# x is added to the early part of y by VectorE instead of TensorE, twelve idle matmuls are dropped, and the stage's entries are spread to its end

## The chip, the cores and the metric

The kernel runs on one core of a Trainium2 chip. The metric is the device time of one execution in microseconds (us); the time before is the median of three runs. Where a time inside an execution is given, it counts from the first instruction of the profiled execution.

Engines in the profile: PE is TensorE (matmuls), PEld its weight loads, DVE VectorE, ACT ScalarE, POOL GpSimd, SP SyncE. "Granted clock" is the share of its full clock that TensorE was given at that moment.

## The reference

```python
# attention with a causal window of 64, 8 batches x 8 heads, 576 rows, 64 columns
scores = scale * np.matmul(q, k.transpose(0, 1, 3, 2))
mask = (rel >= 0) & (rel < 64)
attn_out = softmax(where(mask, scores, -1e9)) @ v
x = attn_out.transpose(0, 2, 1, 3).reshape(8, 576, 512)
# spectral mix: 64 modes, a complex 512 x 512 matrix for each
X = np.fft.rfft(x, axis=1)
Yr = einsum('bmd,mde->bme', Xr, w_r) - einsum('bmd,mde->bme', Xi, w_i)
Yi = einsum('bmd,mde->bme', Xr, w_i) + einsum('bmd,mde->bme', Xi, w_r)
Y[:, :64] = Yr + 1j * Yi
y = np.fft.irfft(Y, n=576, axis=1)
u = x + y
out = u + np.maximum(u @ w_ch, 0.0)
```

## The kernel before

**The stream of weights.** The mode matrices `w_r` and `w_i` are 127 loads of 1 MB each (the imaginary part of mode 0 isn't needed), cast to 512 KB of bf16 on the way by GpSimd's DMA queue (`load_w`). They start during the attention and run until shortly before the output. Every load, numbered 0 to 126, is used by one call of `half(i)` (L533): 16 matmuls with the weights as the stationary operand and the modes of all batches, XQ, as 16 moving columns. The results gather in two PSUM banks, `psys`, and every eight modes are copied to `YT` (the first 48 modes, "early", 96 rows of real and imaginary parts) or to `YTl` (the last 16, "late", 32 rows).

**The slots.** After the attention, the loop variable `now` counts slots: `half(now)`, then `issue(now)` (L506), which issues the loads for which a buffer is free, then the functions that were put into `work[now]`. The order on PE, POOL, DVE and ACT is that of the program (`manual_schedule`). Slots 0 to 94 end with the last early mode: `S_I` is 95. Slots 95 to 124 (`T_I` is 125) are the stage that is changed. Halves 125 and 126 come behind it, in the tail.

**The buffers.** `ring` (L491) holds 14 places for weights: five of `wlate`, eight of `wmid` and, as the only one without a pool, the first half of XQ once its modes are used up (`view(XQ, ...)`). Work that needs room takes a place with `claim` and returns it with `give`; `taken` counts what is claimed in each slot, and `issue` doesn't issue a load that would leave too little for a later claim. `claim` prefers the XQ place when it is free.

**The stage's entries.** With the early modes known, the inverse transform of the early part is done while the late weights stream in. For each pair p of batches, 60 entries in all:
- `turn_first(b)` transposes a batch's `YT` (four matmuls of 128 columns), and VectorE copies it to `Yp[b]`; `channel_first(b)` multiplies it by `w_ch` (four matmuls of 512 columns), and ScalarE copies that.
- `make_u(p, t)` for row tiles t = 0 to 3: for the two batches, the inverse transform of the early part (one matmul each, stationary `trigI`), and x added to it by a second matmul each with a unit matrix (`ident_bf`, L727). ScalarE copies the 128x1024 sum to `U`. For t < 2, `U` is a claimed place; for t = 2 and 3 it lies over x itself, in rows of one batch that are read up to t = 3, so both copies are made after the last tile of x is read (`late_u`).
- `add_z(p, t)`: the same with the `w_ch` rows, and VectorE adds the result to `Z0`, which holds x @ w_ch from earlier slots.
- `last_tile(p, x)`: the last 64 rows of both batches at once, for Z (VectorE adds) and for u (ScalarE copies; x is added by a matmul with a permuted unit matrix).
- `drop(p)` returns two claimed places.

`make_u`, `add_z` and `last_tile` share two PSUM tiles of two banks each (`ps_e`, tag `pse`). L797 spreads the entries evenly over slots 95 to 122. In slots 122 and 123 six idle matmuls each (L840) use a further `ps_e` tile, `psd`.

**The tail.** The PSUM of the stage is given up and taken over by the tail's tiles. `lay` puts `Z0` of two tiles into PSUM, two idle matmuls follow, half 125, six idle matmuls, half 126 (L929 to L934). Then the late part is turned, multiplied by `w_ch`, and for each of 18 slot tiles added to Z (`late_rows`), rectified on ScalarE, completed by the late part of u, added to `U` on VectorE (`final`, L916) and written out by SyncE's queue.

Of the kernel before, what the change touches and what calls it, by code (L numbers as in the profile page):

```python
# [9 lines left out]
FP32 = mybir.dt.float32  # L10
# [3 lines left out]
ALU = mybir.AluOpType  # L14
# [6 lines left out]
def view(ap, off, dims):  # L21

    return bass.AP(ap.tensor, ap.offset + off, [list(ap.ap[0])] + [list(d) for d in dims])
# [3 lines left out]
def kernel(  # L27
# [10 lines left out]
    nc = tc.nc  # L38
    B, H, S, D = q.shape
    NM = moe_w_r.shape[0]  # L40
    DM = moe_w_ch.shape[0]
# [3 lines left out]
    NT = 5  # L45
# [23 lines left out]
    ident_bf = consts.tile([128, 128], BF16, name="ident_bf")  # L69
    ident_r = consts.tile([128, 128], FP32R, name="ident_r")  # L70
    trigF = consts.tile([128, NT, 2 * NM], BF16, name="trigF")
    x_sb = keep.tile([128, B // 2, 2 * NT, DM], BF16, name="x_sb")
# [3 lines left out]
    def block(b, t):  # L76

        return t if b % 2 == 0 else (t + 1) % NT

    def x_rows(b, t, n=128):  # L80
        return x_sb[:n, b // 2, (b % 2) * NT + block(b, t), :]
# [32 lines left out]
    NLOAD = 2 * NM - 1  # L114
# [5 lines left out]
    def load_w(i, pool, tag, wt=None):  # L120
        m, im = divmod(i + (i > 0), 2)
        if wt is None:
            wt = pool.tile([128, NC, DM], BF16, name="wt", tag=tag)
        src = moe_w_i if im else moe_w_r
        nc.gpsimd.dma_start(out=wt, in_=src[m].rearrange("(p c) e -> p c e", c=NC))  # L125
        wtiles[m, im] = wt
# [28 lines left out]
    with tc.tile_pool(name="tmpf", bufs=1, side="right") as tmp:  # L155
# [6 lines left out]
        for t0, t1 in ((0, 3), (3, NT)):  # L162
            n = t1 - t0
            mt = tmp.tile([128, 2, n * NM], FP32, name="mtf")
            nc.vector.tensor_tensor(out=view(mt, 0, [[NM, n], [1, NM]]), in0=view(mo, 0, [[0, n], [1, NM]]),
                                    in1=view(to, t0, [[1, n], [0, NM]]), op=ALU.mult)
# [188 lines left out]
    nw = 0  # L355
# [38 lines left out]
    with tc.manual_schedule(engines={mybir.EngineType.PE, mybir.EngineType.Pool}):  # L394
# [11 lines left out]
        for b in range(1, B):  # L406
            start = -(-9 * (b - 1) // 2)
# [12 lines left out]
        for w in range(NWIN + 1):  # L420
# [5 lines left out]
            n = len(todo)  # L426
# [16 lines left out]
            if w in (NWIN - 4, NWIN - 1):  # L443
                i = (B - 2) % 2 if w == NWIN - 4 else (B - 1) % 2
# [4 lines left out]
            if w in (NWIN - 4, NWIN):  # L449
                i = (B - 2) % 2 if w == NWIN - 4 else (B - 1) % 2  # L450
# [17 lines left out]
    E0 = 96  # L468
# [16 lines left out]
    turns_bf = late2.tile([128, 64, 2], BF16, name="turns_bf")  # L485
# [5 lines left out]
    ring = [(i, wlate, "wl", None) for i in range(LW)]  # L491
# [4 lines left out]
    S_I = 2 * L0 * MG - 1  # L496
    T_I = NLOAD - 2
    work = {}
    taken = [0] * (NLOAD + 1)

    def put(i, f, delta=0):
        work.setdefault(i, []).append(f)
        for j in range(i, NLOAD + 1):
            taken[j] += delta

    def issue(i):  # L506
        nonlocal nw
        while nw < NLOAD:
            ring.sort(key=lambda r: (max(r[0], i), r[1] is not None, r[0]))
            if ring[0][0] > i:  # L510
                return
            held = [r[0] for r in ring if r[0] > i] + [nw]
            if any(sum(x > j for x in held) + taken[j] > places for j in range(i, nw + 1)):
                return
            _, pool, tag, ap = ring.pop(0)
            load_w(nw, pool, tag, ap)
            ring.append((nw, pool, tag, ap))
            nw += 1

    now = 0  # L520

    def claim(name, dtype=FP32R):
        ring.sort(key=lambda r: (r[0], r[1] is None))
        r = ring.pop(0)
        assert r[0] <= now, (name, now, ring)
        if r[1] is None:
            return r[3].rearrange("p c e -> p (c e)").bitcast(dtype).rearrange("p (a e) -> p a e", a=2), r
        return r[1].tile([128, 2, DM], dtype, name=name, tag=r[2]), r

    def give(c):  # L530
# [2 lines left out]
    def half(i):  # L533
        m, im = divmod(i + (i > 0), 2)
        w = wtiles.pop((m, im))
        psy = psys[m // MG % 2 if m < NM - 1 else 0]
        off = (m % MG) * NC * 2 * B if m < NM - 1 else 0
        own = m % MG == 0 or m == NM - 1
        for e in range(NC):
            for c in range(NC):  # L540
                nc.tensor.matmul(out=view(psy, off + 2 * B * e, [[1, 2 * B]]),  # L541
                                 lhsT=w[:, c, 128 * e:128 * e + 128],
                                 rhs=XQ[:, m // HM, c, :, 1 - im:3 - im, m % HM],
                                 start=own and not im and e == 0 and c == 0,
                                 stop=c == NC - 1 and (im == 1 or m == 0), skip_group_check=True)
        if (im or not m) and (m % MG == MG - 1 or m == NM - 2):
            g, n = m // MG, m % MG + 1
            for ri in range(2 if m < NM - 1 else 0):
                if g < L0:
                    dst = view(YT, g * 2 * MG + ri * MG, [[E0, NC], [NC * E0, B], [1, n]])  # L550
                else:
                    dst = view(YTl, (g - L0) * 2 * MG + ri * MG, [[B * R, NC], [R, B], [1, n]])
                evac(dst, view(psy, ri, [[2 * B, NC], [2, B], [NC * 2 * B, n]]), ri)
# [144 lines left out]
    Yp, U = {}, {}  # L698

    def spent(k):  # L700

        return view(YT, 2 * DM * k, [[DM, 2], [1, DM]])

    def turn_first(b):
        Yp[b] = claim("Yb") if b < B - 2 else (spent(b - B + 2), None)
        psa = ps_a.tile([128, NC, 128], FP32R, name="psa")
        for e in range(NC):
            nc.tensor.transpose(out=psa[:E0, e, :], in_=YT[:, b, e, :], identity=ident_r)
        nc.vector.tensor_copy(out=Yp[b][0][:E0, 0, :], in_=psa[:E0].rearrange("p c e -> p (c e)"))

    def channel_first(b):
        psw = ps_a.tile([128, DM], FP32, name="psw")
# [5 lines left out]
    def first_rows(ps, b, t, k, x):  # L718

        parts = [(b, 128 * t)] if t < NT - 1 else [(b, 513), (b + 1, 512)]  # L720
        for n, (bb, o) in enumerate(parts):
            last = n == len(parts) - 1
            nc.tensor.matmul(out=ps, lhsT=trigI[:E0, o:o + 128], rhs=Yp[bb][0][:E0, k, :],  # L723
                             start=n == 0, stop=last and not x)
        if x:
            perm = ident_bf if t < NT - 1 else view(turns_bf, 0, [[1, 128]])
            nc.tensor.matmul(out=ps, lhsT=perm, rhs=x_rows(b, t), start=False, stop=True)  # L727

    def add_z(p, t):
        ps = ps_e.tile([128, 2, DM], FP32, name="pse", tag="pse")  # L730
# [2 lines left out]
        z = Z0[:, 4 * p + t]  # L733
        nc.vector.tensor_tensor(out=z, in0=ps, in1=z, op=ALU.add)  # L734

    late_u = []

    def make_u(p, t):
        ps = ps_e.tile([128, 2, DM], FP32, name="psf", tag="pse")
        for j in range(2):  # L740
            first_rows(ps[:, j, :], 2 * p + j, t, 0, True)
        if t < 2:
            U[4 * p + t] = claim("U", FP32)[0]
            nc.scalar.copy(out=U[4 * p + t], in_=ps)
            return
        U[4 * p + t] = x_sb[:, p, NT * (t - 2) + t - 2:NT * (t - 2) + t + 2, :].bitcast(FP32).rearrange(
            "p (j h) e -> p j (h e)", j=2)
        late_u.append((4 * p + t, ps))
        if t == 3:
            for s, q in late_u:  # L750
                nc.scalar.copy(out=U[s], in_=q)
            late_u.clear()

    def last_tile(p, x):
        ps = ps_e.tile([128, 2, DM], FP32, name="psg", tag="pse")
# [16 lines left out]
    items = []  # L772

    def first_of(b, k):
        if b < B:
            items.append((lambda: (turn_first, channel_first)[k](b), 1 - k if b < B - 2 else 0))

    def step(f, *a, delta=0):
        items.append((lambda: f(*a), delta))
# [4 lines left out]
    for p in range(NP):  # L784
        for t in range(3):
            step(add_z, p, t)
            step(make_u, p, t, delta=t < 2)
        first_of(2 * p + 2, 0)
        step(make_u, p, 3)
        first_of(2 * p + 2, 1)  # L790
        step(add_z, p, 3)
        step(last_tile, p, False)
        step(last_tile, p, True)
        step(drop, p, delta=-2 if p < NP - 1 else 0)
        first_of(2 * p + 3, 0)
        first_of(2 * p + 3, 1)
    for k, (f, delta) in enumerate(items):  # L797
        put(S_I + k * (T_I - 2 - S_I) // len(items), f, delta)
    places = len(ring)

    def out_of(s):
# [6 lines left out]
    def idle(o, n):  # L808
        for _ in range(n):
            nc.tensor.matmul(out=o, lhsT=ident_bf, rhs=view(trigF, 0, [[1, DM]]), start=True, stop=True)  # L810

    E = mybir.EngineType
    with tc.manual_schedule(engines={E.PE, E.Pool, E.DVE, E.Activation}):
# [16 lines left out]
        with ExitStack() as pe:  # L830
            ps_a = pe.enter_context(tc.tile_pool(name="ps_a", bufs=1, space=PSUM, reuse_waits="tile"))
            ps_e = pe.enter_context(tc.tile_pool(name="ps_e", bufs=2, space=PSUM, reuse_waits="tile"))
            for now in range(S_I, T_I):
                half(now)
                issue(now)
                for f in work.get(now, []):
                    f()
                if T_I - 3 <= now < T_I - 1:
                    psd = ps_e.tile([128, 2, DM], FP32, name="psd", tag="pse")
                    idle(psd[:, 0, :], 6)  # L840
        now = T_I
        assert nw == NLOAD

# [7 lines left out]
        for h in range(2):  # L851
            left = [[4 * (2 * h + k) + t for t in range(4)] for k in range(2)]
            for _ in range(8):
# [6 lines left out]
                k = 1 - kind[-2] if len(kind) > 1 and kind[-2] is not None else (0 if not kind else 1)  # L860
                k = k if left[k] else 1 - k
# [58 lines left out]
        def pool(name, stack=p2, **kw):  # L920
# [15 lines left out]
                              in_=view(psys[0], 0, [[2 * B, NC], [2, B], [1, 2]]))  # L936
# [58 lines left out]
```

## Time and profile before

| | us |
|---|---|
| median of 3 runs | 431.09 |
| the three runs | 431.09, 430.18, 436.92 |
| the profiled execution's own time | 434.36 |
| its span, first to last instruction | 432.3 |
| PE busy | 355.8 (82%) |
| PEld busy | 234.6 (54%) |
| DVE busy | 186.1 (43%) |
| ACT busy | 160.9 (37%) |
| POOL busy | 91.6 (21%) |
| mean granted clock of TensorE | 0.791 |

The profiled execution is one execution; its time is compared with nothing but itself and the median of the runs. Busy shares are means over stages with different limits. In the view by slices each digit is the busy share of a fortieth of the span in tenths (9 is 90% or more); PEclk is the granted clock in tenths. In the chain of waits a row is the start, the length and the work that the end of the program followed from at that time: a transfer from its issue to its landing, or instructions of an engine. In the view by groups a row is line, engine, operation, tiles, shape and count, then busy us, mean ns of one, and the engine's idle time before it. "x16" is a count of instructions, and a matmul's length in the records holds its way through the array, so that successive ones overlap.

### The profile page before, as it was taken

The numbers are of one execution on the slowest core, as the hardware profiler recorded it, in microseconds if no ns is written. First come the engines' busy times: TensorE is split into PE (matmuls) and PEld (weight loads), VectorE is DVE, ScalarE is ACT, GpSimd is POOL, SyncE is SP. The second block draws the span as 40 slices with busy tenths as digits, with TensorE's granted clock in tenths as the row PEclk, the third lists the DMA queues.
The fourth block names the chain that finished last, engine by engine and source line by source line (L and its number), as shares of the span: only waits on it lengthen the run. The fifth ranks groups of instructions, "written<-read, shape, count | busy, mean of one in ns | idle before, by whom it ended". The sixth has DMA issues, their size and how long they took to land.

```text
span 432.3 us, 11457 instructions
## 1 busy us (share of the span) xinstructions
PE 355.8 (82%) x5148; PEld 234.6 (54%) x5167; DVE 186.1 (43%) x340; ACT 160.9 (37%) x252; POOL 91.6 (21%) x174
## 2 busy tenths in 40 slices
PE   6989998999989667595867768677879899999982
PEld 2555665666654567373645545455546555655431
DVE  5466866776763202173334332111114523351685
ACT  4485866866754100041211120101124222331672
POOL 6131321331111404331221212212212110300000
PEclk9999999999997555597656565765659955899896
DMA  8999999999999999999999999999999999992598
GB/s 143 212 214 214 212 213 213 212 213 213 213 213 203 191 214 180 257 213 213 213 213 214 214 213 213 214 215 213 213 213 213 214 214 213 213 213 50 214 349 313
DMA packets 30352, 91.96 MB, mean 213 GB/s; under 512 B 2784, under 2 KB 2784, under 8 KB 30304
## 3 DMA queue, kind: packets, MB, share of 16 engines
q0 software_dynamic: 25344, 81.80, 95.3%
q1 hardware_dynamic: 4960, 9.44, 5.8%
q8 instruction: 40, 0.66, 0.5%
q14 instruction: 8, 0.07, 0.0%
HBM read 162.53 MB, written 9.44 MB: 398 GB/s over the span
## 4 chain that ended last, share of the span: by engine, by line
PE 45%; DMA 37%; DVE 8%; issue 5%; ACT 3%; POOL 1%; DVEq 0%; POOLq 0%; ACTq 0%
DMA wt<-in_moe_w_r_dram 13%; DMA wt<-in_moe_w_i_dram 12%; DMA XQ<-in_moe_w_r_dram 9%; PE pso L318 6%; PE psy L541 6%; PE pst L221 5%; PE psv L238 3%; PE psx L340 3%; DVE x_sb L326 3%; PE pss L275 2%; DMA wch<-in_moe_w_ch_dram 2%; PE pss L374 2%; PE pss L876 2%; PE pss L294 2%; PE psf L723 2%
## 5 line engine op out<-in xcount | busy, mean ns | idle before, releaser
L541 PE MATMUL psy<-XQ,wt 128*128 128x16 bf16 x1680 | 64.7, 191 | 33.3 <-DMA wt<-in_moe_w_i_dram 16.0
L541 PEld LDWEIGHTS <-wt 128*128 128x128 bf16 x1680 | 55.6, 104 | 64.4 <-DMA wt<-in_moe_w_i_dram 27.4
L682 PE MATMUL psz<-wch,xT 128*128 128x512 f32 x144 | 63.7, 584 | 5.6 <-DMA wch<-in_moe_w_ch_dram 5.6
L685 ACT CAST Z<-psz 128x1024 fp32r<-128x1024 f32 x18 | 18.2, 1012 | 101.0 <-PE psz L682 87.0
L676 DVE CAST xT<-pxt 128x1024 fp32r<-128x1024 bf16 x18 | 22.0, 1225 | 71.8 <-PE pxt L671 71.7
L125 POOL DMA_DIRECT2D wt<-in_moe_w_r_dram x54 | 29.1, 540 | 82.1 <-DMA wt<-in_moe_w_r_dram 34.4
L125 POOL DMA_DIRECT2D wt<-in_moe_w_i_dram x51 | 27.6, 542 | 84.8 <-DMA wt<-in_moe_w_i_dram 38.9
L300 ACT ACTIVATE et<-pss 128x512 bf16<-128x512 f32 x72 | 39.2, 600 | 13.4 <-PE pss L294 12.3
L682 PEld LDWEIGHTS psz<-wch,xT 128*128 128x128 f32 x144 | 36.2, 278 | 11.5 <-issue 5.7
L318 PE MATMUL pso<-vt,et 128*64 128x65 bf16 (+1 forms) x576 | 33.1, 206 | 4.0 <-DVE x_sb L326 3.1
L734 DVE TENSOR_TENSOR Z<-pse,Z 128x1024 fp32r<-128x1024 f32 x16 | 19.6, 1224 | 33.9 <-PE pse L723 33.9
L318 PEld LDWEIGHTS <-et 128*64 128x64 bf16 (+1 forms) x576 | 22.7, 111 | 16.0 <-issue 8.0
L326 DVE TENSOR_TENSOR x_sb<-pso,rcp 128x640 bf16<-128x640 f32 x32 | 26.3, 822 | 0.9
L275 PE MATMUL pss<-band,ident_bf 64*64 64x512 bf16 x160 | 21.2, 410 | 1.4 <-ACT et L300 1.4
L59 DVE COPY vT<-pst 128x768 bf16<-128x768 bf16 x16 | 15.3, 957 | 13.5 <-PE pst L221 13.5
L909 ACT ACTIVATE pss<-pss 128x1024 f32<-128x1024 f32 (+1 forms) x18 | 17.3, 960 | 5.5 <-PE pss L885 4.8
L59 DVE CAST YT<-psy 128x256 fp32r<-128x256 f32 x6 | 2.5, 424 | 38.5 <-PE psy L541 38.5
L294 PE MATMUL pss<-qT,kT 64*64 64x128 bf16 (+1 forms) x640 | 15.6, 218 | 0.6 <-issue 0.6
L58 ACT COPY vt<-psv 128x768 bf16<-128x768 bf16 x16 | 12.9, 808 | 8.5 <-PE psv L238 8.4
L671 PE MATMUL pxt<-ident_bf,x_sb 128*128 128x128 bf16 x144 | 16.0, 281 | 0.0
L238 PE MATMUL psv<-ident_bf,vT 128*128 128x128 bf16 (+1 forms) x160 | 15.5, 226 | 0.4 <-DVE vT L59 0.4
L58 ACT COPY qT<-pst 128x768 bf16<-128x768 bf16 x16 | 12.9, 813 | 6.7 <-PE pst L221 6.7
(177 smaller groups left out, 530.0 us busy)
## 6 DMA issues: line engine op xcount, KB each, us to landing
wt<-in_moe_w_r_dram POOLq DMA_DIRECT2D x54, 512.0 KB, 19.1
wt<-in_moe_w_i_dram POOLq DMA_DIRECT2D x51, 512.0 KB, 19.1
rk<-in_k_dram POOLq DMA_DIRECT2D x8, 576.0 KB, 9.4
rq<-in_q_dram POOLq DMA_DIRECT2D x8, 576.0 KB, 13.4
rv<-in_v_dram POOLq DMA_DIRECT2D x8, 576.0 KB, 12.0
out_dram<-U SPq DMA_DIRECT2D x7, 512.0 KB, 3.6
out_dram<-x_sb SPq DMA_DIRECT2D x7, 512.0 KB, 3.2
XQ<-in_moe_w_i_dram POOLq DMA_DIRECT2D x4, 512.0 KB, 12.8
```

The source lines that it names most:

```text
L58: return nc.scalar.copy(out=o, in_=i)
L125: nc.gpsimd.dma_start(out=wt, in_=src[m].rearrange("(p c) e -> p c e", c=NC))
L221: nc.tensor.transpose(out=ps[64 * hh:64 * hh + 64, c, :], in_=src[:, hh, (c0 + c) * D:(c0 + c + 1) * D], identity=ident_bf)
L238: nc.tensor.transpose(out=ps[r0:r0 + n, i, :], in_=vT[:, g, t0:t0 + n], identity=ident_bf)
L275: nc.tensor.matmul(out=pss[(2 * w + hh) % 3][64 * half:64 * half + 64, :], lhsT=ident_bf[pp, pp], rhs=view(band[pp], 128 * half, [[0, WIN ...
L294: nc.tensor.matmul(out=pss[(2 * w + hh) % 3][64 * half:64 * half + 64, col:col + nq], lhsT=kTs[b % 2][pp, g, 64 * kb:64 * kb + 64], rhs=qT ...
L300: nc.scalar.activation(out=et[:, hh, :], in_=pss[(2 * w + hh) % 3], func=ACT_F.Exp, scale=EX_SCALE)
L318: nc.tensor.matmul(out=pso[po, hh, block(b, i // 2) * VW:block(b, i // 2) * VW + D + 1], lhsT=et[pk, hh, col:col + 64], rhs=vt[pk, 1 - f % ...
L326: nc.vector.tensor_tensor(out=view(x_sb, b * NT * DM + g * D, [[4 * D, 2], [DM, NT], [1, D]]), in0=view(pso, 0, [[512, 2], [VW, NT], [1, D]]),
L541: nc.tensor.matmul(out=view(psy, off + 2 * B * e, [[1, 2 * B]]), lhsT=w[:, c, 128 * e:128 * e + 128], rhs=XQ[:, m // HM, c, :, 1 - im:3 - ...
L676: nc.vector.tensor_copy(out=o, in_=i)
L682: nc.tensor.matmul(out=psz[s][:, j, :], lhsT=xts[s % 2][0][:, j, 128 * c:128 * c + 128], rhs=wch[:, c, :], start=(c == 0), stop=(c == NC - 1))
```

## The change

- `make_u` no longer adds x by a matmul. VectorE adds x (bf16, from `x_sb`) to the PSUM tile and writes `U`, for every t; ScalarE's copies and the list `late_u` go. For t = 2 and 3, `U` now lies over the two row tiles of x of both batches with the indices 2(t-2) and 2(t-2)+1.
- `turn_first`'s copy moves from VectorE to ScalarE.
- The XQ place leaves the ring as soon as it is next in turn and a load beyond number 95 is to be issued (`first_u`); it becomes `U[0]`, which so needs no claim. `claim` takes places of pools alone.
- The twelve idle matmuls of slots 122 and 123 go.
- The entries are spread over slots 95 to 124 (`T_I - S_I` instead of `T_I - 2 - S_I`).

```diff
@@ issue
+            if ring[0][1] is None and nw > S_I:
+                first_u.append(ring.pop(0)[3])
+                for j in range(i, NLOAD + 1):
+                    taken[j] += 1
+                continue
@@ claim
-        assert r[0] <= now, (name, now, ring)
-        if r[1] is None:
-            return r[3].rearrange("p c e -> p (c e)").bitcast(dtype).rearrange("p (a e) -> p a e", a=2), r
+        assert r[0] <= now and r[1] is not None, (name, now, ring)
@@ turn_first
-        nc.vector.tensor_copy(out=Yp[b][0][:E0, 0, :], in_=psa[:E0].rearrange("p c e -> p (c e)"))
+        nc.scalar.copy(out=Yp[b][0][:E0, 0, :], in_=psa[:E0].rearrange("p c e -> p (c e)"))
@@ first_rows
         if x:
-            perm = ident_bf if t < NT - 1 else view(turns_bf, 0, [[1, 128]])
-            nc.tensor.matmul(out=ps, lhsT=perm, rhs=x_rows(b, t), start=False, stop=True)
+            nc.tensor.matmul(out=ps, lhsT=view(turns_bf, 0, [[1, 128]]), rhs=x_rows(b, t), start=False, stop=True)
@@ make_u
+    def pair_rows(p, k, n):
+        return view(x_sb, (p * 2 * NT + k) * DM, [[(NT + 1) * DM, 2], [1, n * DM]])
+
     def make_u(p, t):
         ps = ps_e.tile([128, 2, DM], FP32, name="psf", tag="pse")
         for j in range(2):
-            first_rows(ps[:, j, :], 2 * p + j, t, 0, True)
-        if t < 2:
-            U[4 * p + t] = claim("U", FP32)[0]
-            nc.scalar.copy(out=U[4 * p + t], in_=ps)
-            return
-        U[4 * p + t] = x_sb[:, p, NT * (t - 2) + t - 2:NT * (t - 2) + t + 2, :].bitcast(FP32).rearrange(
-            "p (j h) e -> p j (h e)", j=2)
-        late_u.append((4 * p + t, ps))
-        if t == 3:
-            for s, q in late_u:
-                nc.scalar.copy(out=U[s], in_=q)
-            late_u.clear()
+            first_rows(ps[:, j, :], 2 * p + j, t, 0, False)
+        if p + t == 0:
+            U[0] = first_u.pop().rearrange("p c e -> p (c e)").bitcast(FP32).rearrange("p (a e) -> p a e", a=2)
+        else:
+            U[4 * p + t] = claim("U", FP32)[0] if t < 2 else pair_rows(p, 2 * (t - 2), 2).bitcast(FP32)
+        nc.vector.tensor_tensor(out=U[4 * p + t], in0=ps, in1=pair_rows(p, t, 1), op=ALU.add)
@@ entries
-            step(make_u, p, t, delta=t < 2)
+            step(make_u, p, t, delta=t < 2 and p + t > 0)
...
-        put(S_I + k * (T_I - 2 - S_I) // len(items), f, delta)
+        put(S_I + k * (T_I - S_I) // len(items), f, delta)
@@ slots 95 to 124
-                if T_I - 3 <= now < T_I - 1:
-                    psd = ps_e.tile([128, 2, DM], FP32, name="psd", tag="pse")
-                    idle(psd[:, 0, :], 6)
```

More of the change, by code (lines that the diff above doesn't have):

```diff
@@ L518, in issue @@
             nw += 1
+    first_u = []
     now = 0
@@ L734, in add_z @@
         nc.vector.tensor_tensor(out=z, in0=ps, in1=z, op=ALU.add)
-    late_u = []
+    def pair_rows(p, k, n):
+        return view(x_sb, (p * 2 * NT + k) * DM, [[(NT + 1) * DM, 2], [1, n * DM]])
     def make_u(p, t):
```

## The prediction

> **What bounds the kernel now.** I read the page's slices first: where the transfers are the bound, and which clock TensorE had.
>
> ```profile
> PEclk9999999999997555597656565765659955899896
> DMA  8999999999999999999999999999999999992598
> ```
>
> A slice is 10.8 us. The transfers are full up to slice 36, while TensorE's granted clock swings. Then the chain of waits around the changed stage:
>
> ```profile
> 327.32 19.53 DMA XQ<-in_moe_w_r_dram
> 346.85 0.05 issue
> 346.89 0.65 PE psy L541 x16
> ...
> 389.18 1.29 PE psd L810 x6
> ...
> 394.66 1.29 PE pss L810 x6
> 395.96 0.44 PE psy L541 x16
> ```
>
> Up to 346.85 the weights set the end of the chain. From there to 396.40 it holds no transfer: TensorE has fallen behind. The windows view, cut at the edges at which the granted clock changes (always multiples of 3.41 us apart), shows why and by how much:
>
> ```profile
> 343.40:346.81 3.41, 2.28 (x26) 1.27 (x24) 1.91 (x2) 0.96 (x1) 0.00 (x0) 1.00 1.08 216
> 346.81:350.23 3.42, 3.34 (x22) 2.08 (x24) 0.00 (x0) 1.58 (x2) 0.53 (x1) 0.50 1.07 214
> 367.30:370.71 3.41, 3.41 (x26) 2.15 (x26) 1.23 (x2) 0.00 (x0) 1.01 (x2) 0.50 1.07 215
> 377.54:380.95 3.41, 2.97 (x39) 1.95 (x39) 1.58 (x2) 1.34 (x2) 0.00 (x0) 1.00 1.05 210
> 392.50:393.00 0.50, 0.50 (x10) 0.46 (x7) 0.24 (x1) 0.00 (x0) 0.00 (x0) 1.00 0.10 16
> 393.00:394.60 1.60, 1.60 (x23) 1.04 (x22) 0.15 (x1) 0.35 (x1) 0.00 (x0) 1.00 0.00 0
> 398.02:401.43 3.41, 2.82 (x18) 1.42 (x17) 2.39 (x4) 2.75 (x4) 0.00 (x0) 1.00 0.00 0
> 401.43:404.84 3.41, 3.41 (x10) 1.86 (x11) 2.64 (x3) 1.33 (x2) 0.00 (x0) 0.50 0.73 267
> ```
>
> Columns: length, busy time of PE, PEld, DVE, ACT, POOL, then clock, DMA share, GB/s. The last weights are in by 393.0, yet the last half starts at 395.8 and ends at 396.4: TensorE is about 2.9 us late, and that is all that work in this stage can win. It lost this time at half clock: eight slots from 346.89 to 372.14 (3.16 us each) against weights every 2.43 us (load 107 landed at 346.85, load 126 near 392.95, 19 apart). At full clock it made up 11 slots in 23.66 us (372.14 to 395.80, 2.15 each).
>
> What sets the clock? For each 3.41 us window I summed the columns that passed the array, weighted by the share of rows and columns used, over what the granted clock allows (2,381 per us at full clock: six idle matmuls of 512 in 1.29 us). After 150 us, windows at full clock whose share was 0.11 to 0.37 were followed by half clock (343.40 with 0.37, 398.02 with 0.36, whose 32-row matmuls keep PE busy but fill little); those from 0.39 up kept it, and one at 0.36 (377.54). At half clock, shares of 0.68 to 0.86 brought the full clock back (367.30: 0.68), but several of 0.60 to 0.76 did not (363.88: 0.70). A "busy" PE is not enough: the seven windows from 346.81 are 91 to 100% busy and six of them changed nothing.
>
> The operations concerned, from the groups of this stage (315 to 396.4 us):
>
> ```profile
> L734 DVE TENSOR_TENSOR Z<-pse,Z 128x1024 fp32r<-128x1024 f32 x16 | 19.6, 1224 | 33.9 <-PE pse L723 33.9
> ...
> L727 PE MATMUL psf<-x_sb,ident_bf 128*128 128x512 bf16 x24 | 10.9, 456 | 0.0
> ```
>
> **The change, part by part.** *Matmuls of x.* Each of 16 `make_u` loses two of 512 columns (32; the trace kept 24 records). The chain charges one 0.45 at half clock, 0.23 at full: 7 us of TensorE at full clock, 14 at half, none beyond the 2.9 us on the path that sets the end.
>
> *VectorE.* 16 additions of 128x1024 from PSUM and bf16 replace 16 ScalarE copies of 1.01 us. Nearest rows: 1.22 us (PSUM with fp32, same size) and 0.82 us for 640 elements of PSUM (L326), 1.31 scaled to 1,024. I take 1.22. A slot with `add_z` and `make_u` then has 2.45 us of VectorE in 2.43, and with two PSUM buffers the next slot's matmuls, and the half behind them, can wait. Slots with `turn_first`, `channel_first` or `last_tile` between let it catch up (a pair of batches: eight such adds, 9.8, and 0.7, in 18.2 us). Against that, TensorE no longer waits for ScalarE's copies of U (L744 and L751: 1.6 us in five waits). Price: from a gain of 1.6 us to a lateness of 1 that doesn't add up; I take 0.3 late, as the waits named were early in a pair and made up. `turn_first`'s copy on ScalarE (0.58 for its like, L716, against 0.69) rides beside that; ScalarE loses 16 copies.
>
> *Buffers.* XQ's half leaves the ring at load 107 rather than when U is claimed. By the planner's own rules the last load is then due after half 119 (before: 120), and no late load is due less than six slots (14.6 us) ahead. In the timeline load 126 was issued at 383.51, 9.4 us ahead, and the transfers stayed full. So 0 us at the stream's end; if that cover went, each late slot would cost 2.43.
>
> *Idle matmuls and the spread.* Twelve of 0.215 us go (2.6 us at full clock), and the entries run to slot 124 instead of 122: slot 123 gets `add_z` and half a `last_tile`, slot 124 three matmuls of 512 whose ScalarE copy (0.58) the first `lay` must wait for, since it takes over that PSUM. Of DMAs, only the weight loads' slots move, as said.
>
> *The clock: the deciding part.* Columns of a pair, weighted: `add_z` 3,072, `make_u` 3,072 and x 4,096, `last_tile` 2,048, `channel_first` 3,072, `turn_first` 768, halves 256 a slot. Before: 17.9 thousand in 7 slots (17.0 us, 40.5 thousand at full clock): 0.44. After: 13.9 thousand in 7.5 slots (18.2 us, 43.4 thousand): 0.32. That is under every share that kept the full clock, so I expect half clock for most of the stage; there it is 0.64, at the edge of what brings it back. At half clock TensorE just keeps pace: a `make_u`/`add_z` slot falls from 3.28 us (363.10 to 366.38) to 2.40; a pair, from 7 x 3.16 = 22.1 us less 8 x 0.44 = 18.6, against 18.2. So I put it 0.3 to 1.3 us late at slot 124.
>
> The last stretch at half clock, from the landing of load 124 (392.95 - 2 x 2.43 = 388.1): half 0.5, three matmuls 1.28, wait for the copy 0.9 (drain 0.2, copy 0.58, two handovers), four `lay` 1.71, two idle 0.85, half 0.5, six idle 2.56, last half 0.5: 8.8 us, so an end at 397.2 to 398.2. Dense work from 391 on fills a window, whose edge may fall anywhere from 394.3 to 397.7, and what is left then runs twice as fast: some 0.8 us saved on average. I take 396.9 against 396.4: **+0.5 us** on the profiled execution, 434.9 of 434.36. The gain of 2.9 us is eaten by the clock.
>
> The median before is 431.09, 3.3 below the profiled execution (span 432.3 plus 2.1 around it), nearly its 2.9 us of lateness. I read that as runs in which TensorE was on time; that is inferred from times alone. If the change makes the lateness regular, it shows against the median: I forecast **434.6 us**, 0.8% slower. A measurement of this kernel can tell about 2% from no change.
>
> **Rivals.** *A: on time at full clock.* With dense slots keeping the share up, the last half ends 0.55 us after its load, at 393.5: 431.5 by the profiled execution, and 430.2 if the half-clock window at 401.43 also goes (its ten matmuls would take 0.2 less each, 2 us, of which I take 1.3, as VectorE is busy for 2.64 of its 3.41 us and hides part). For it: 377.54 kept the clock at 0.36, and less work is less to be late with. Against: the sum of 0.32. The Trainium skill ("TensorE: Matmul & The Clock Gate", the sections "What's actually happening" and "Why this matters for your kernels") has the clock fall after an idle window of some 3.4 us and rise after a busy one. By that rule no window here is idle, the clock would hold, and this rival would be the outcome; the trace disagrees, with 343.40 two thirds busy before its fall and six busy windows at half clock. Chance 0.25, in 429.5 to 432.5.
>
> *B: the tail stays slow.* Without a lift before the last half, the tail starts at half clock. The chain's TensorE pieces from 396.4 to 424 sum to 22 us of 28, so a 3.41 us window at half clock does half its work and costs up to 1.3 us. Shares in the tail are 0.36 and 0.47 to 0.53 at full clock, so most windows would hold it; four more low windows cost 5.2 us, and from there the run is over 2% slower: 440 to 446 with four to nine. For it: two such falls (398.02, 421.91) and a run of 436.92 before. Against: dense idle and `lay` matmuls just ahead of the tail. Chance 0.14.
>
> *C: VectorE or the buffers hold the stage*, one or two slots late: 437 to 439. Chance 0.04; against it, VectorE is busy for 28.6 of this stage's 81.4 us now (42.7 after: 16 x 1.22 more, 8 x 0.69 less), and a load is issued 19.5 us ahead (the chain's row at 327.32), eight landings.
>
> *D: no effect*, as the stage hides under the transfers and the clock does as before: 431. Chance 0.07.
>
> **The numbers.** Forecast 0.50 (433 to 436.5). Range 429.5 to 439.5: A's end below, C's above; B is left out, with a little of the rest. Faster by over 2% (below 422.5) would need more than the stage has to give: 0.01. Slower by over 2% (above 439.7) is B: 0.14. Within: 0.85.
>
> **What would show it.** Right: granted clock at half in most windows from 330 to 390, the six idle matmuls ahead of the last half (L810) near 2.6 us instead of 1.29, the last half 3 to 4 us after its load. Wrong: those windows at full clock, or the last half within 1 us of the load (A); clock at half after 405 (B); DMA share below 1 before 385 or VectorE full in a window with PE waiting for it (C). The additions at L734's 1.22 us would confirm their price.

## The result, and the profile after

| | before | after |
|---|---|---|
| median, us | 432.24 (6 runs) | 435.89 (6 runs) |
| range, us | 429.9 to 439.36 | 434.69 to 437.17 |
| ratio after to before | | 1.0115, 95% interval 1.0078 to 1.0152 |
| profiled execution, its time / span | 434.36 / 432.3 | 437.17 / 435.2 |
| mean granted clock, profiled execution | 0.791 | 0.756 |
| DVE busy / ACT busy, us | 186.1 / 160.9 | 199.1 / 149.7 |

The change makes the kernel about 1.1% slower. The ratio leaves out executions that took over 1.5% more than the fastest of the same kernel, which the medians and ranges hold; by the medians the loss is 0.8%. The profile of the changed kernel is of the slowest of its six executions. First the slices of the page of the changed kernel (10.9 us each):

```profile
PEclk9999999999985555596656566566685686656998
DMA  8999999999999999999999999999999999990598
```

The transfers are as full as before up to slice 36. The clock of slices 31 to 33 has moved (5, 6, 8 where it was 9, 9, 5), and ahead of the tail, in slices 34 to 37, it has fallen: 6, 6, 5, 6 where it was 5, 8, 9, 9. Now the chain of waits of the changed kernel around the last weights (start, length, work):

```profile
387.64 1.24 DVE x_sb L751
...
388.97 1.24 DVE x_sb L751
...
390.25 1.23 PE psg L727 x2
...
393.53 0.59 ACT x_sb L758
...
394.17 1.22 PE psf L872 x2
395.39 0.85 PE pss L872 x2
396.25 0.88 PE pss L809 x2
397.12 0.47 PE psy L545 x16
397.60 2.56 PE pss L809 x6
400.16 0.46 PE psy L545 x16
```

The entries of slots 122 to 124 (two additions of x, the last tile, ScalarE's copy of it) run until 394.1; only then do `lay` (L872), two idle matmuls (L809), half 125 (397.12), six idle matmuls in 2.56 us instead of 1.29, and the last half follow. It ends at 400.62; before, at 396.40. The windows of the changed kernel, cut at the edges of its granted clock and at the end of the transfers (length; busy PE, PEld, DVE, ACT, POOL; clock, DMA share, GB/s):

```profile
325.10:328.51 3.41, 2.66 (x25) 1.37 (x22) 3.41 (x5) 0.00 (x0) 0.99 (x2) 1.00 1.08 217
359.23:362.64 3.41, 1.80 (x31) 1.28 (x27) 2.36 (x2) 0.00 (x0) 0.00 (x0) 1.00 1.06 214
372.88:376.30 3.42, 2.62 (x39) 1.73 (x36) 1.80 (x2) 1.00 (x2) 1.41 (x3) 1.00 1.07 216
383.12:386.54 3.42, 3.42 (x38) 2.25 (x37) 3.24 (x4) 0.00 (x0) 0.00 (x0) 0.50 1.07 214
393.36:393.90 0.54, 0.00 (x0) 0.00 (x0) 0.00 (x0) 0.37 (x1) 0.00 (x0) 0.50 0.04 8
393.90:396.78 2.88, 2.61 (x6) 1.50 (x7) 0.00 (x0) 0.22 (x1) 0.00 (x0) 0.50 0.00 0
396.78:400.19 3.41, 3.41 (x30) 1.59 (x29) 0.00 (x0) 0.00 (x0) 0.00 (x0) 0.50 0.00 0
400.19:403.60 3.41, 2.54 (x28) 1.82 (x25) 0.99 (x3) 0.71 (x2) 0.00 (x0) 1.00 0.00 0
```

The last weights are in by 393.9, 0.9 us later than in the execution before. The three windows at full clock are each the last before a fall: their shares of columns, summed as in the prediction, are 0.32, 0.23 and 0.29. The limit isn't sharp: the window from 355.82 has 0.31 and kept the full clock. The one of 396.78 has 0.92, and the full clock comes back at 400.19, when the last half is nearly done. The additions themselves, from the groups of 315 to 400.5 us:

```profile
L737 DVE TENSOR_TENSOR Z<-pse,Z 128x1024 fp32r<-128x1024 f32 x16 | 19.5, 1221 | 31.2 <-PE pse L727 31.2
...
L751 DVE TENSOR_TENSOR x_sb<-psf,x_sb 128x1024 f32<-128x1024 f32 x8 | 9.8, 1224 | 3.1 <-PE psf L727 3.0
L751 DVE TENSOR_TENSOR U<-psf,x_sb 128x1024 f32<-128x1024 f32 x7 | 8.5, 1219 | 0.7 <-PE psf L727 0.7
```

They cost 1.22 us each, like `add_z`'s, also where output and input lie over each other.

### The profile page after: what moved, and what is told of

The parts are those of the page before. It is cut to its first block, busy times and chain, and to the rows that moved or that the text cites. A ratio compares the mean times of both kernels' runs of the same rounds, so it can differ in the third digit from the quotient of the medians.

```text
span 435.2 us, 11380 instructions
## 1 busy us (share of the span) xinstructions
PE 356.0 (82%) x5109; PEld 236.4 (54%) x5123; DVE 199.1 (46%) x348; ACT 149.7 (34%) x244; POOL 91.4 (21%) x174
## 4 chain that ended last, share of the span: by engine, by line
PE 44%; DMA 37%; DVE 9%; issue 5%; ACT 2%; POOL 1%; DVEq 0%; another core or an unknown queue 0%; POOLq 0%; ACTq 0%
DMA wt<-in_moe_w_r_dram 31%; PE pso L318 6%; PE psy L545 5%; PE pst L221 5%; DMA XQ<-in_moe_w_r_dram 5%; PE psv L238 3%; PE psx L340 3%; PE pss L275 3%; DVE x_sb L326 3%; DMA wch<-in_moe_w_ch_dram 2%; PE psz L686 2%; PE pss L294 2%; PE pss L374 2%; PE pss L872 2%; DVE vT L59 2%
## 5 line engine op out<-in xcount | busy, mean ns | idle before, releaser
L545 PE MATMUL psy<-XQ,wt 128*128 128x16 bf16 x1744 | 68.5, 192 | 37.5 <-DMA wt<-in_moe_w_i_dram 18.0
L545 PEld LDWEIGHTS <-wt 128*128 128x128 bf16 x1744 | 59.3, 106 | 72.4 <-DMA wt<-in_moe_w_i_dram 31.1
L125 POOL DMA_DIRECT2D wt<-in_moe_w_i_dram x54 | 29.1, 539 | 97.0 <-DMA wt<-in_moe_w_i_dram 42.4
L686 PEld LDWEIGHTS psz<-wch,xT 128*128 128x128 f32 x144 | 37.1, 285 | 11.1 <-issue 5.2
L318 PE MATMUL pso<-vt,et 128*64 128x65 bf16 (+1 forms) x576 | 34.1, 210 | 4.0 <-DVE x_sb L326 3.2
L325 DVE RECIPROCAL rcp<-pso 128x10 f32<-128x10 f32 x32 | 6.9, 214 | 18.6 <-PE pso L318 18.3
```

The source lines that it names most:

```text
L318: nc.tensor.matmul(out=pso[po, hh, block(b, i // 2) * VW:block(b, i // 2) * VW + D + 1], lhsT=et[pk, hh, col:col + 64], rhs=vt[pk, 1 - f % ...
L686: nc.tensor.matmul(out=psz[s][:, j, :], lhsT=xts[s % 2][0][:, j, 128 * c:128 * c + 128], rhs=wch[:, c, :], start=(c == 0), stop=(c == NC - 1))
```

## The experiments

Three numbers tell the runs apart. *Lateness* of a half is the start of its first weight load less the landing of its load's last packet; it and the *half clock* (microseconds of half clock in the 75 us ahead of the last landing) come from the one profiled execution. A half that starts as soon as its load is there shows about 0.3 us, since the chain of waits counts the landing that much behind the last packet. The 2.9 and 5.65 us that the expectations below give for halves 124 and 125 of the changed kernel count from a packet that isn't the load's last; from the last they are 2.3 and 5.1 us. The ratio is that of many executions to the kernel before on the same chip.

| | ratio (95% interval) | median, us | profiled, us | lateness of half 124 / 126, us | half clock, us |
|---|---|---|---|---|---|
| before | 1 | 431.97 to 433.43 | 434.36 | 3.8 / 2.64 | 28.9 |
| after | 1.0115 (1.0078 to 1.0152) | 435.89 | 437.17 | 2.3 / 5.68 | 51.1 |
| e1 old spread | 1.001 (0.9959 to 1.006) | 431.28 | 431.02 | 0.3 / 0.35 | 36.7 |
| e2 old spread, twelve idles | 1.0027 (0.9984 to 1.0071) | 431.78 | 432.39 | 2.0 / 0.78 | 33.5 |
| e3 before, no twelve idles | 1.0002 (0.9952 to 1.0052) | 430.9 | 429.67 | 0.3 / 0.84 | 26.9 |
| e4 one pad | 1.0114 (1.0051 to 1.0177) | 434.64 | 434.64 | 4.2 / 4.63 | 34.1 |
| e5 half 125 ahead | 1.0083 (1.0034 to 1.0132) | 434.94 | 433.87 | 2.4 / 4.61 | 54.0 |
| e6 no tail idles | 1.0119 (1.0029 to 1.0208) | 436.98 | 436.72 | 2.4 / 2.83 | 54.5 |
| e7 x on TensorE | 1.0158 (1.0067 to 1.0249) | 438.21 | 438.98 | 5.8 / 9.21 | 37.5 |
| e8 last pair on TensorE | none | 438.71 | 441.67 | 5.9 / 9.24 | 57.9 |
| e9 one slot less | 1.0038 (0.9994 to 1.0081) | 433.26 | 429.30 | 0.3 / 0.77 | 47.0 |
| e10 four slots less | 0.9988 (0.9945 to 1.0032) | 430.65 | 430.51 | 0.3 / 1.21 | 44.3 |
| e11 two pads | 1.0045 (0.9998 to 1.0091) | 432.89 | 436.14 | 4.8 / 6.55 | 22.6 |
| e12 old spread, idles, two pads | 0.9963 (0.9923 to 1.0002) | 429.33 | 428.51 | 1.5 / 0.36 | 4.3 |

**e1: the old spread alone.**

```diff
-        put(S_I + k * (T_I - S_I) // len(items), f, delta)
+        put(S_I + k * (T_I - 2 - S_I) // len(items), f, delta)
```

> The changed kernel with its entries in slots 95 to 122 as before; the twelve idle matmuls stay out. Three theories. S, the spread: TensorE is late at the end because entries lie in slots 123 and 124 and the first lay waits for their copies. Without them two slots (4.9 us) are free, the last half ends within 1.5 us of its load, and the time falls by 4 to 5 us below the changed kernel, to 430 to 432 us. C, the clock: what costs is half clock from a thin stage; two empty slots thin the end further, the tail starts at half clock, and the time is 433 to 436. V, VectorE's two additions a slot over two PSUM tiles hold TensorE back: lateness in the middle stays, the end catches up in two slots: 431 to 434.

The loss is gone: 1.001. The chain of this run has the tail's first work behind the weights again:

```profile
369.96 16.81 DMA wt<-in_moe_w_i_dram
386.77 0.05 issue
386.82 0.66 PE psy L545 x16
387.48 1.04 PE psf L872 x2
388.52 0.85 PE pss L872 x2
389.37 0.88 PE pss L809 x2
390.25 0.47 PE psy L545 x16
390.72 0.09 issue
390.82 1.24 PE pss L809 x5
392.06 0.50 PE psy L545 x16
```

Half 124 waits for its load here, as do halves 119 to 121 and 123: TensorE keeps pace in these slots though the clock is at half from 377.0 on. The same `lay` and idle matmuls, at half clock up to 390.7, start right behind half 124 (386.82), not 2.9 us after its start (391.27 to 394.17 in the changed kernel), and the last half starts 0.35 us after its load landed, with 36.7 us of half clock in the stage. So S holds: all that the change does besides the spread (additions on VectorE, copies moved, the buffer of `U[0]`, idle matmuls dropped) costs nothing that 0.5% can show.

**e2: old spread and the twelve idle matmuls.** To e1 this adds

```diff
+                if T_I - 3 <= now < T_I - 1:
+                    psd = ps_e.tile([128, 2, DM], FP32, name="psd", tag="pse")
+                    idle(psd[:, 0, :], 6)
```

> The changed kernel with both the old spread and the twelve idle matmuls: what is left of the change is the addition on VectorE, the copy on ScalarE and the buffer of U 0. S: as the run with the old spread alone, within 1 us, since the idle matmuls lie in free slots. C: the idle matmuls raise the clock ahead of the tail, 1 to 3 us faster than the run without them. V: no faster than that run, 431 to 434.

1.0027 against 1.001: no difference. The twelve idle matmuls alone neither lift the clock enough to be seen nor cost anything that these intervals (some 0.5% each way) would show. They make half 123 2.4 us late, and by the last half 0.78 us of that is left.

**e3: the kernel before without them.** The same three lines taken out of the kernel before.

> The kernel before without its twelve idle matmuls, nothing else. C: the last slots hold only the halves, the share of columns falls under 0.36 at slot 123, the tail starts at half clock: 1 to 3 us slower than the kernel before. S and V: TensorE was 2.9 us late in the profile and has 2.6 us less to do: 0 to 2.6 us faster.

1.0002. Both sides of the expectation lie next to no effect, and neither is borne out: TensorE's lateness of the one profile of before was no fixed quantity to be won (here it is 0.84 us). The interval reaches some 2.2 us each way, so a smaller effect would not show.

**e4: TensorE's columns put back as idle matmuls.**

```diff
         for j in range(2):
+            idle(ps[:, j, :], 1)
             first_rows(ps[:, j, :], 2 * p + j, t, 0, False)
```

> The changed kernel with one idle matmul of 512 columns ahead of each of make_u's 32 matmuls, in the same PSUM tile: TensorE streams the columns that the x matmuls streamed, and nothing else is as before. C: the share is 0.42 again, fewer half-clock windows between 320 and 395 us than the changed kernel's 16 of 22, and the time is the same or up to 4 us lower although TensorE has 7 to 14 us more to do. S and V: more work for an engine that is late: 1 to 4 us slower.

Half clock falls from 51.1 to 34.1 us, as C says, yet the time stays at 1.0114. In the profile the clock was low from 374.8 to 388.5, just where the added matmuls made slots 120 to 123 late (1.7 us at half 120, 4.6 at half 123). The amount of columns that before had is not enough; with an interval of 1.0051 to 1.0177 this run neither proves nor refutes the clock.

**e5: half 125 ahead of `lay`.**

```diff
+        half(T_I)
         lay(0)
         lay(1)
         idle(bank(3, 0), 2)
-        half(T_I)
```

> The changed kernel with half 125 ahead of the two lay and the two idle matmuls, spread to slot 124 as in the change. Theory W, the wait: with entries in slot 124, the first lay waits for the last entry's copy (1.2 us idle in the profile of the changed kernel), and half 125 and all behind it is queued behind that. Half 125 then starts within 3.5 us of its load instead of 5.65, but half 126 still lies behind lay: 0 to 1.5 us faster than the changed kernel. Theory L, the load: what counts is the work that lies between the landing of load 124 and half 126, not its order: the same time within 0.8 us.

Half 125 is 1.4 us late instead of 5.1, the last half 4.61 instead of 5.68. The time, 1.0083, can't be told from the change's 1.0115. In the profiles the order of the queue is worth 1.1 us of the last half's lateness; the work itself still lies ahead of it.

**e6: no idle matmuls in the tail.**

```diff
-        idle(bank(3, 0), 2)
         half(T_I)
-        idle(bank(3, 0), 6)
```

> The changed kernel without the eight idle matmuls between lay and half 126. L: at half clock they take 3.4 us of the path; the last half starts 2 to 3.4 us earlier and the time falls to 432 to 434. C, the clock: they are what lifts the clock ahead of the tail; without them the tail's first 3 to 7 us run at half clock, which costs 1.5 to 4 us and eats that: 434.5 to 437.

C holds. The last half comes 2.83 us behind its load, 2.85 less than in the changed kernel, but from its start to the end of the span it takes 39.06 us instead of 35.68. The windows of this run show the tail's beginning (columns as above):

```profile
395.71:399.00 3.29, 2.86 (x31) 2.26 (x27) 0.27 (x1) 0.05 (x1) 0.00 (x0) 0.50 0.00 0
399.00:402.00 3.00, 2.74 (x13) 1.25 (x14) 1.39 (x2) 2.03 (x3) 0.00 (x0) 0.50 0.00 0
402.00:405.00 3.00, 3.00 (x13) 1.48 (x10) 2.63 (x4) 1.33 (x2) 0.00 (x0) 0.50 0.36 135
405.00:408.40 3.40, 3.40 (x14) 2.17 (x13) 1.01 (x1) 1.70 (x2) 0.00 (x0) 0.50 0.92 341
```

12.7 us at half clock, which the changed kernel doesn't have behind 400.19. The eight idle matmuls pay for their place by lifting the clock: without them the ratio is 1.0119, no better than the change's 1.0115.

**e7: x on TensorE again, with the spread.**

```diff
-        nc.vector.tensor_tensor(out=U[4 * p + t], in0=ps, in1=pair_rows(p, t, 1), op=ALU.add)
+        nc.scalar.copy(out=U[4 * p + t], in_=ps)
```

and the x matmul, and `turn_first`'s copy on VectorE, as before.

> The changed kernel with x added by TensorE and copied by ScalarE as before, turn_first's copy on VectorE as before: of the change, the spread to slot 124, the missing idle matmuls of slots 122 and 123 and the buffer of U 0 are left. Theory S alone (the spread costs whoever adds): as slow as the changed kernel, 434 to 437, since TensorE has 14 us more at half clock. Theory V with S (VectorE's seven additions in a row, 9.6 of 10.7 us busy, pace slots 120 to 123): 430.5 to 433, VectorE below 70% there. C (the thin stage): at most 433, with fewer half-clock windows than the changed kernel.

V falls. From 380 to 391 us VectorE is busy for 9.19 us in the changed kernel and for 3.06 here (first fence the changed kernel, second this run; columns as above):

```profile
380.00:391.00 11.00, 10.89 (x81) 6.42 (x81) 9.19 (x8) 0.00 (x0) 0.00 (x0) 0.50 1.06 213
```

```profile
380.00:391.00 11.00, 10.08 (x58) 5.31 (x60) 3.06 (x3) 3.05 (x4) 0.00 (x0) 0.50 0.93 186
```

Yet the last half is 9.21 us late instead of 5.68, and the median 438.21 lies over the changed kernel's 435.89, and over S's 434 to 437 too. Under this spread at half clock TensorE is the bound. The spread, not the addition, is the harmful part. That the addition on VectorE softens it is what the two profiles say (9.21 and 5.68 us); the times don't show it, since 1.0067 to 1.0249 overlaps the change's interval.

**e8: the last pair alone on TensorE.** The edit of e7 for `p == NP - 1` only, without `turn_first`'s copy.

> The changed kernel with the last pair of batches alone (four make_u, slots 120 to 122) adding x on TensorE and copying on ScalarE. V: VectorE has four additions of 1.22 us fewer in slots 120 to 123, half 124 starts under 2 us after its load instead of 2.9, and the time falls by 1 to 2.5 us. S and L: TensorE has eight matmuls more (3.4 us at half clock) in the slots where it is late: 0 to 2 us slower.

Its four executions lie between 429.32 and 441.67 us, too far apart for a ratio, and its profile is the slowest of them. In that, half 124 is 5.9 us late, the opposite of V's forecast; on the time it is inconclusive.

**e9 and e10: other spreads.** `T_I - 1 - S_I` and `T_I - 4 - S_I` in the line of e1.

> The changed kernel with its entries in slots 95 to 123: half of the spread. L: room of one slot (2.4 us) comes back between the last entry and the last half, whose lateness falls from 5.7 us to 2 to 3.5, and the time lies between the two spreads, 432.5 to 434.5. If instead the one step that counts is that slot 124 is no longer empty (W), it is that of the old spread, 430.5 to 432.5.

> The changed kernel with its entries in slots 95 to 120, denser than before. L: the last half is on time already with the old spread (0.35 us behind its load), so nothing more is won: 430 to 432.5. C: five slots that hold the halves alone thin the end out, the tail starts at half clock with 7 us or more of it: 433 to 436.

The ratios of 2, 1 and 0 slots free are 1.001, 1.0038 and 1.0115, and of four 0.9988. The order is that of L, though e9's interval reaches to both neighbours, and its profile is of its fastest execution, so its small lateness need not be typical. e10 shows what slack does: its halves 118 to 121 are 3.7 to 4.6 us late, the empty slots catch that up, and half 123 starts as soon as its load is there. C's fear for the tail isn't borne out: 1.9 us of half clock there.

**e11: two pads.** `idle(ps[:, j, :], 2)` in place of e4's 1.

> The changed kernel, spread to slot 124, with two idle matmuls ahead of each of make_u's 32 matmuls (64 idle matmuls, 13.8 us at full clock). C: the share of columns of a make_u slot at full clock is 0.6 instead of 0.3, full clock holds once it is reached, a slot then takes 2.2 us of its 2.4, the last half starts within 2.5 us of its load, and the time falls to 430 to 433.5. L without the clock: 64 matmuls more in slots that are late, 437 to 444.

64 matmuls more than the changed kernel, and it is faster: median 432.89 against 435.89, ratio 1.0045 against 1.0115. The intervals touch (1.0091 and 1.0078), so the size is uncertain, but L without the clock asked for 437 to 444 and fails. Half clock is 22.6 us. The profiled execution is one of its slower ones (436.14): the clock fell at 376.1, behind a window with a share of 0.29, and came back at 386.3, and what was late then stayed late, as the spread leaves no free slot.

**e12: the addition on VectorE, old spread, twelve idle matmuls, two pads.**

> The addition on VectorE with the old spread and the twelve idle matmuls, and two idle matmuls ahead of each of make_u's: meant to hold the full clock through the stage and into the tail. C: under 20 us of the last 75 at half clock, the last half within 1 us of its load, 429 to 431.5, and runs closer together than those of before. L: as the run with the old spread and idle matmuls, 430.5 to 433, if late work is caught up in the two free slots; 433 to 436 if not.

The slices' clock line of this run:

```profile
PEclk9999998999999655597666665656669999999998
```

From 320.15 to 422.55 us the clock is full without a break, at shares of 0.37 to 0.74 in all windows but the last (0.02). The end of the chain around the last half:

```profile
389.26 0.23 PE pss L810
389.49 0.05 issue
389.54 0.64 PE psy L545 x16
390.18 1.29 PE pss L810 x6
391.47 0.50 PE psy L545 x16
```

The six idle matmuls take 1.29 us, and the last half is 0.36 us late. It is the fastest version here, 429.33 us median, and clearly faster than the changed kernel; its interval against the kernel before (0.9923 to 1.0002) just reaches no difference, and 1.0027 for the same without pads (e2) has an interval that overlaps it.

## Why the prediction was right, and which step was not

The forecast was 434.6 us, in a range of 429.5 to 439.5; the median is 435.89, slower by 1.1% where 0.8% was forecast. Point by point:

- *VectorE's additions, 1.22 us; no price to speak of.* Right: 1.22, and 1.001 with the old spread (e1). Set against them were 1.6 us of waits for ScalarE's copies of U; those were waits of weight loads, while matmuls waited 0.8 us (L744 and L751), and in the changed kernel they wait 0.8 us for the additions instead. Rival C, VectorE holding the stage, isn't the cause of the loss: e7 loses no less with VectorE busy for 3.06 of 11 us. Rival D, no effect, falls with the interval of the result.
- *Buffers, no price.* Right: the transfers stay full to the end.
- *The clock at half for most of the stage.* Right: 51.1 of the last 75 us, and falls behind windows with shares of 0.23 to 0.32. Rival A (on time at full clock) didn't come about. By the Trainium skill's rule ("TensorE: Matmul & The Clock Gate", "What's actually happening") the clock falls behind an idle window; here it fell behind windows with PE busy for 1.80 to 2.66 of 3.41 us, so the trace disagrees again.
- *The last stretch.* Its mechanism was right and its size too small. Forecast was an end of the last half at 396.9; it was 400.62, 3.7 us later. Three terms make that up: half 124 was put 0.3 to 1.3 us late and was 2.3 (1.5 us over the middle); the stretch from there was put at 8.8 us less 0.8 for a lift of the clock, and took 9.35 (391.27 to 400.62) with the lift at its very end (1.35); load 124 landed 0.8 later than estimated (388.9 against 388.1), which came from ahead of the stage (load 66 already landed 0.8 later than before). So the last half came 5.68 us behind its load, not the 3 to 4 that were named as the sign. The tail then gave 1.3 us back: 34.6 us from 400.62 to the end of the span, against 35.9 before, whose tail had a window at half clock (rival B didn't come about: the clock is full from 400.19 to 430.91). Hence 435.2 of span.
- *The total.* That it is met within 1.3 us is in part luck. For the profiled execution 434.9 us was forecast and 437.17 came; the median lies 1.3 us below that profile, and the 3.7 and 1.3 us of the last stretch and the tail have opposite signs.
- *"The gain of 2.9 us is eaten by the clock."* This attribution failed. The prediction made the thinner stage the deciding part and priced the spread by slot 124's three matmuls and one wait (2.2 us). The runs show the reverse order: without the spread, a stage with 36.7 us of half clock costs nothing that shows (e1), because slots 123 and 124 hold nothing but their halves and `lay` follows half 124 at once; where there is lateness, such slots catch it up (e2, e10). With the spread, the slots at the end are filled at half clock, and `lay`, eight idle matmuls and two halves come after them. The clock is what makes that stretch long: with two pads TensorE has more to do and the time is lower, by 0.7% of the changed kernel's (e11) and by 0.6% of the same kernel's without pads (e12 against e2), each with an uncertainty of about 0.6% (the two ratios' intervals taken together); one pad (e4) shows no gain. So half clock without the spread was not the loss.
- *The 2.9 us of lateness before as something to be won.* The prediction took the median before for runs in which TensorE was on time. That fits: versions whose last half is at most 1.2 us late (e1, e3, e10) have the median of the kernel before, within their intervals, so there was nothing to win there that would show.
- *Twelve idle matmuls, 2.6 us at full clock.* Taking them out wins nothing that shows, and putting them back costs nothing (e3 and e2). The eight of the tail do matter (e6).

What stays open: whether the spread alone, at full clock, costs anything (e11, with 22.6 us of half clock left, reaches from 0.9998 to 1.0091), and what exactly sets the clock: at half clock windows with shares of 0.6 to 0.76 went both ways, and at full clock some near 0.31.

## What to carry to other kernels

Work that hides under a stream of transfers needs free room behind it, not an even spread to the last slot: whatever is late there, by an engine or by the clock, lies ahead of the tail. Taking matmuls off TensorE can slow the rest of its work: under the same spread half clock was 37.5 of 75 us with x on TensorE (e7) and 51.1 without, and matmuls that compute nothing brought full clock back (33.5 us of half clock in e2, 4.3 in e12). Look at the clock by windows before counting such a removal as a gain. A few idle matmuls can be worth their time where they keep the clock up ahead of a serial tail, and here cost nothing that showed where slots had room.

## What was not expected of the hardware

- The granted clock stayed full for 102 us (e12), at shares of columns of 0.37 to 0.74 up to the window after which it fell, with 64 matmuls that compute nothing; without them it was at half for 33.5 us of the last 75 (e2).
- The stream of weights itself isn't steady from execution to execution. Load 66 landed between 242.5 (e12) and 246.9 us (e8) in the profiled executions, ahead of the stage, where all these kernels do the same; load 26 had landed within 0.2 us (140.5 to 140.7). Some 4 us of difference from there reach the last load (last packet at 390.8 in e12, 395.2 in e8) and limit what one profile can say of 1%. Of the 6.2 us between the profiles of the changed kernel and e1, 2.4 are the stream's (last packets at 393.85 and 391.42).
